# Where a step's router products and scaled output stand beside a batch's list products: one step of a fused attention and expert kernel

## The chip, the cores and the metric

The kernel runs on one core of a Trainium2 chip. The metric is the device time of one execution in microseconds, lower is better. Five engines run side by side, each through its own list of instructions in order: PE (TensorE, matrix products), DVE (VectorE), ACT (ScalarE), POOL (GpSimd) and SP (SyncE, which here only issues DMAs). They meet through semaphores. Matrix products write to PSUM banks, which DVE and ACT read; POOL works on SBUF and also issues the indirect DMAs that gather and scatter rows.

## What is computed

The reference is a linear attention with decay, followed by a mixture of experts with two levels of routing. Cut to what matters:

```python
state = gamma[None, :, None, None] * state + np.einsum('bhd,bhe->bhde', k[:, :, t], v[:, :, t])
y[:, :, t] = scale * np.einsum('bhd,bhde->bhe', q[:, :, t], state)
...
g_idx = np.argmax(x @ w_group, axis=1)             # 4 groups
e_idx = np.argmax(xg @ w_expert[g], axis=1)        # 4 experts in the group
h = np.maximum(xg[mask_e] @ w1[g, e], 0.0)
out[tok_idx] = combined[:, None] * (h @ w2[g, e])  # combined: the two softmax weights
```

Sizes: batch 4, 8 heads, 768 positions, head width 64. The attention's output is 3072 rows of 512, each of which goes through one of 16 experts (512 to 1024 to 512).

## The kernel before

**Stages.** The attention is done in 12 steps (`attention`, loop over i), each with two chunks of 128 positions. A step computes the scores of the next step (`score_mm`, L235, masked on DVE into `pf` at L247), the share of the carried state in the output (`state_out`, L286), the share of the step's own keys and values (`value_out`, L299) and the new state (`state_mm`, L261). Both shares are summed in two PSUM banks `op`, of a ring of two with the tag "mid". `out_x` (L311, DVE) multiplies them by the decay into `xt`, the scaled output. `logits_mm` (L319, PE) multiplies the `xt` of the step before by the router's weights, ACT copies the result to `ls` (L324), and `select_mm` (L332) brings it into the order of tokens. `trans_mm` (L345) transposes `xt`, ACT copies it to `xr` (L353), and SP stores it into the array `xd` in HBM (L356).

**Routing.** Six batches of four chunks are routed, beside the attention, by `route`: the choice of group and expert on DVE (L385 to L403), ranks by matrix products on PE (L436, L438), weights on DVE and POOL. From the places, `spread` makes one-hot marks `hot` (L485, DVE) and entries `yT` (L501, POOL). `tally` (L522, PE: four list products for each batch) adds them up in the PSUM bank `log`, and DVE adds that to `lists` (L529). The fourth batch is tallied in step 10, and this completes the first list for the 2048 rows so far (expert 0, called early).

**After that tally**, `beside(10, 5)` makes the first list's ids and weights with DVE (`tokens`: L534, L535, written to `mt`), issues the gather of these rows from `xd` on POOL (`gather`, L775, into `xg`), and prepares a sum `pre` for later (`known`, L541). In step 11 `xtrans` transposes the gathered rows on PE (L793). It stands behind step 11's value products and ahead of the router products of step 10, the ranks of the fifth batch and the transposes. Thereafter the first expert's layers start (L840), and fifteen further rounds over experts follow.

**What sets the order.** Nothing is scheduled by a planner: the order on each engine is that in which the Python code writes the instructions. Between engines only the tracked dependencies count. Two of them matter here. `state_out` of step 11 writes into the `op` banks of step 10, so it waits until L311 has read them. And L793 waits for the gather's DMA. `vs` (L192) and `wl` (L753) in the rows are POOL's other work, the scaled values and the low part of the split weights; `wf` at L739 is a load of weights by SP.

Of the kernel before, what the change touches and what calls it, by code (L numbers as in the profile page):

```python
# [106 lines left out]
class Kernel:  # L107
# [961 lines left out]
    def attention(self, extra, beside):  # L1069

        self.setup()
        for o in "qB0 kB0 vB0 q1 k1 v1 q2 k2 w0 c0".split():
            n, us = int(o[-1]), {"A": (0,), "B": (1,)}.get(o[1], (0, 1))
            if o[0] == "c":
                self.nc.sync.dma_start(self.rest, self.a_cst[:, C_REST:])
            elif o[0] == "w":
                self.nc.sync.dma_start(self.wr[:, :, 0:20], self.a_wr.rearrange("p (k e) -> p k e", k=4))
            else:
                self.load(o[0], n, us)

        def scores(i, u):
            if i < NS2:
                self.score_mm(i, u)
                self.score_mask(i, u)

        scores(0, 0)
        self.keys_mm(0, (0,), (self.log, self.log))
        self.vprep(0)
        self.decay_first()
        self.outs(0)  # L1090
        self.value_out(0, 0)
        scores(0, 1)
        self.keys_mm(0, (1,), (self.log, self.log))
        self.state_mm(0, 0)
        self.load("v", 2)
        self.load("k", 3)
        for i in range(NS2):
            last = i == NS2 - 1
            if i == 10:
                self.route_steps(99, True)  # L1100
                self.spread(3)
            if not last:
                self.vprep(i + 1)
            beside(i, -1)
            if i + 1 < NC:
                self.decay_next(i + 1)
            beside(i, 0)
            if i:
                if i > 2:
                    self.outs(i)  # L1110
                if i > 1:
                    scores(i + 1, 0)
                if i % 2 and not last:
                    self.select_late()
                if i in (5, 7, 9):
                    self.tally()
                if i > 2:
                    self.state_out(i, 0)
                if last:
                    self.select_late()  # L1120
                if i > 1:
                    self.state_out(i, 1)
                if i < NS2 - 2:
                    self.select_late()
                if i % 2 == 0:
                    self.route_steps(99, True)
                if i > 1:
                    scores(i + 1, 1)
            self.load("q", i + 3)
            self.load("v", i + 3)  # L1130
            if i % 2:
                self.route_steps(99)
            beside(i, 2)
            if i:
                self.value_out(i, 0)
            self.value_out(i, 1)
            if i:
                self.state_mm(i, 0)
            self.state_mm(i, 1)
            self.state_copy(i)  # L1140
            if i == 10:
                self.select_late()
                self.tally()
                beside(i, 5)
            beside(i, 4)
            if i:
                self.logits_mm(i - 1, 1 if last or i % NC == NC - 2 or i + 1 in KEYED else 2)
            self.out_x(i)
            if i < 2:
                scores(i + 1, 0)  # L1150
                scores(i + 1, 1)
            if i in (4, 6, 8):
                self.spread(i // 2 - 2)
            if last:
                self.route_steps(1, True)
                self.route_steps(99)
            beside(i, 1)
            if not last:
                banks = (self.log, self.sh[0]) if i < 2 else None
                if i == 0:  # L1160
                    self.keys_mm(1, (0,), banks)
                    self.outs(1)
                    self.state_out(1, 0)
                    self.state_out(1, 1)
                    self.keys_mm(1, (1,), banks)
                else:
                    self.keys_mm(i + 1, banks=banks)
                if i == 1:
                    self.outs(2)
                    self.state_out(2, 0)  # L1170
                self.load("k", i + 4)
            if i:
                late = i + 1 in KEYED or i % NC == NC - 2
                self.trans_mm(i - 1, late=late)
                if late:
                    self.late = i - 1
                else:
                    del self.st[i - 1]
            beside(i, 3)
            if i % 2 and not last:  # L1180
                self.route_steps(99, True)
            if i == 1:
                self.const_pieces()
            if last:
                extra(i)
            if i and i % 2 == 0:
                self.steps.append(self.route(i // 2 - 1))
            if not last:
                extra(i)
# [261 lines left out]
```

## Time and profile before

| | |
|---|---|
| time, median of 3 runs | 407.74 us (406.2 to 408.5) |
| the profiled execution | 407.63 us, of which the span from the first to the last instruction is 405.9 us |
| PE busy | 391.5 us, 96% of the span |
| DVE busy | 295.5 us, 73% |
| ACT busy | 223.4 us, 55% |
| POOL busy | 169.1 us, 42% |
| mean granted clock of TensorE | 0.989 of full speed |

Times inside the trace count from the span's start. The attention takes the first 107 us or so, the experts the rest. A granted clock of 1.00 is 2.4 GHz and 0.50 is 1.2 GHz; the mean over a stretch tells how much of it lay at the lower level.

### The profile page before, as it was taken

Reading aid. Unit: us, or ns where it says so; the run is one execution under the profiler, and the core shown is the slowest. Engines: PE = TensorE matmul, PEld = TensorE weight load, DVE = VectorE, ACT = ScalarE, POOL = GpSimd, SP = SyncE. Lnnn points to the kernel's source line nnn. Section 1 sums busy time; section 2 is a strip of 40 time slices with the busy share of each in tenths; the row PEclk is TensorE's granted clock in tenths of the full one; section 3 lists DMA queues with packets and bytes.
Section 4 is the critical chain, followed back from the end, with each engine's and each line's share of the span. In section 5 each row is a group of like instructions: output and inputs, shape, how many; then the busy total and the mean of one; then the engine's idle time right before and its main releaser. Section 6 shows DMA issues by size and latency. Waiting matters only on the chain.

```text
span 405.9 us, 13868 instructions
## 1 busy us (share of the span) xinstructions
PE 391.5 (96%) x5809; PEld 326.0 (80%) x5841; DVE 295.5 (73%) x483; ACT 223.4 (55%) x340; POOL 169.1 (42%) x172
## 2 busy tenths in 40 slices
PE   9998999998889999999999999999999999999992
PEld 5888988987769978586979888797887978879792
DVE  4575776867789979886758686777878778788620
ACT  3233535534545656555556666576766767667520
POOL 4551768668374707141507143360523505232001
PEclk9999999999999999999999999999999999999997
DMA  7999899986754997776777787879788897797000
GB/s 265 354 350 351 297 338 332 322 296 183 226 196 163 336 371 256 266 255 247 240 268 263 256 276 265 308 281 307 270 284 309 292 320 270 256 351 261 9 31 36
DMA packets 39507, 107.13 MB, mean 264 GB/s; under 512 B 12116, under 2 KB 12244, under 8 KB 32276
## 3 DMA queue, kind: packets, MB, share of 16 engines
q1 hardware_dynamic: 29760, 93.57, 66.3%
q0 software_dynamic: 9536, 12.63, 9.1%
q8 instruction: 47, 0.77, 0.8%
q14 instruction: 16, 0.13, 0.1%
q10 hardware_dynamic: 148, 0.03, 0.0%
HBM read 94.18 MB, written 13.20 MB: 265 GB/s over the span
## 4 chain that ended last, share of the span: by engine, by line
PE 46%; issue 35%; POOL 12%; DVE 3%; ACT 1%; DMA 1%; POOLq 0%; SPq 0%; ACTq 0%; DVEq 0%
PE hps L840 11%; POOL out L999 6%; PE yps L875 6%; PE op L299 5%; PE sh L235 4%; POOL xg L775 4%; PE yps L922 3%; PE op L286 2%; PE sh L345 2%; PE stp L261 2%; PE yps L925 2%; PE tpx L793 1%; PE sh L220 1%; PE sh L319 1%; PE log L332 1%
## 5 line engine op out<-in xcount | busy, mean ns | idle before, releaser
L753 DVE TENSOR_TENSOR wl<-wf,wh 128x1024 bf16<-128x1024 f32 x120 | 145.3, 1220 | 36.6 <-ACT wh L751 36.3
L751 ACT ACTIVATE wh<-wf 128x1024 f16<-128x1024 f32 (+1 forms) x136 | 133.6, 1002 | 0.3 <-DMA wf<-w2p 0.3
L840 PE MATMUL hps<-xbl,wh 128*128 128x128 f16 (+16 forms) x544 | 128.6, 249 | 0.0
L840 PE MATMUL hps<-xbh,wl 128*128 128x0 bf16 x544 | 125.8, 241 | 0.0
L840 PE MATMUL hps<-xbh,wh 128*128 128x0 bf16 x544 | 125.8, 241 | 0.0
L999 POOL DMA_INDIRECT out<-yo,mt x30 | 39.7, 1322 | 157.3 <-ACT yo L981 119.3
L840 PEld LDWEIGHTS <-wh 128*128 128x128 f16 x1088 | 94.9, 98 | 1.0 <-issue 0.2
L925 PEld LDWEIGHTS <-wh 128*128 128x128 f16 x768 | 47.1, 97 | 22.9
L775 POOL DMA_INDIRECT xg<-xd,mt x30 | 54.2, 1807 | 13.1 <-PE tpx L793 4.5
L845 ACT ACTIVATE hh<-hps 128x256 bf16<-128x256 f32 (+16 forms) x68 | 34.2, 503 | 43.7 <-PE hps L840 43.1
L840 PEld LDWEIGHTS <-wl 128*128 128x128 bf16 x544 | 53.2, 98 | 0.7
L247 DVE TENSOR_TENSOR pf<-sh,tri 128x512 f32<-128x512 f32 x48 | 30.6, 685 | 21.9 <-PE sh L235 8.1
L795 ACT ACTIVATE xbh<-tpx 128x512 bf16<-128x512 f32 (+14 forms) x32 | 16.7, 523 | 48.9 <-PE tpx L793 48.9
L848 DVE SCALAR_TENSOR_TENSOR hl<-hps,hh 128x216 f16<-128x216 f32 (+15 forms) x64 | 36.6, 574 | 4.1 <-ACT hh L845 3.7
L922 PE MATMUL yps<-wh,hl 128*128 128x512 f16 x96 | 36.4, 379 | 0.0
L922 PE MATMUL yps<-wh,hh 128*128 128x512 f16 x96 | 36.4, 379 | 0.0
L922 PE MATMUL yps<-wl,hh 128*128 128x512 bf16 x96 | 36.3, 378 | 0.0
L925 PEld LDWEIGHTS <-wl 128*128 128x128 bf16 x384 | 24.2, 97 | 11.4
L818 DVE TENSOR_TENSOR xbl<-tpx,xbh 128x512 f16<-128x512 f32 (+14 forms) x32 | 19.1, 597 | 18.3 <-ACT xbh L795 18.3
L192 POOL TENSOR_TENSOR vs<-lv,cst 128x512 f32<-128x512 f32 x24 | 24.6, 1046 | 14.0 <-DMA lv<-qkv 10.1
L925 PE MATMUL yps<-hl,wh 128*128 128x108 f16 (+11 forms) x384 | 29.1, 198 | 0.0
L925 PE MATMUL yps<-hh,wh 128*128 128x0 bf16 x384 | 26.6, 190 | 0.0
(194 smaller groups left out, 602.2 us busy)
## 6 DMA issues: line engine op xcount, KB each, us to landing
wf<-w1p SPq DMA_DIRECT2D x28, 1024.0 KB, 7.5
wf<-w2p SPq DMA_DIRECT2D x28, 1024.0 KB, 6.9
lq<-qkv SPq DMA_DIRECT2D x24, 256.0 KB, 5.5
lk<-qkv SPq DMA_DIRECT2D x24, 256.0 KB, 5.4
lv<-qkv SPq DMA_DIRECT2D x24, 256.0 KB, 5.9
xd<-xr SPq DMA_DIRECT2D x22, 256.0 KB, 4.4
wf<-w1p SPq DMA_DIRECT2D x16, 256.0 KB, 5.7
wf<-w2p SPq DMA_DIRECT2D x16, 256.0 KB, 5.5
```

What stands on the lines that cost most here:

```text
L192: self.nc.gpsimd.tensor_tensor(o, v, g, ALU.mult)
L247: nc.vector.tensor_tensor(o, sc, tri, ALU.mult)
L751: nc.scalar.activation(u["wh"][i][:, cs], u["wf"][i][:, cs], AF.Copy)
L753: (eng or nc.vector).tensor_tensor(u["wl"][i][:, cs], u["wf"][i][:, cs], u["wh"][i][:, cs], ALU.subtract)
L775: nc.gpsimd.indirect_dma_start(out=xg[0:r, i, :], out_offset=None, in_=self.xd[0:n, :], in_offset=bass.IndirectOffsetOnAxis(ap=mt[0:r, i, ...
L840: nc.tensor.matmul(o, l[:, k, fs], m, start=(n == 0), stop=(n == 11), skip_group_check=True)
L845: nc.scalar.activation(hh[:, f, 0:W], hv[:, :, 0:W], AF.Relu)
L848: nc.vector.scalar_tensor_tensor(*rest)
L875: nc.tensor.matmul(ps[0:r, :], l[:, k, ts], m[k], start=(n == 0), stop=(n == 23))
L922: nc.tensor.matmul(big, h[:, k, 0:P], w[k], start=(n == 0), stop=(n == 23))
L925: nc.tensor.matmul(o, w[k][:, d * P:d * P + P], m, start=(n == 0 and d == 0), stop=(n == 23), skip_group_check=True,)
L999: s = nc.gpsimd.indirect_dma_start(out=self.out, out_offset=bass.IndirectOffsetOnAxis(ap=mt[0:r, i, 0:1].bitcast(U32), axis=0), in_=yo[0:r ...
```

## The change

In step 10, the list products of the fourth batch with everything that hangs on them (the list sum, the ids and weights, the gather's issue, the prepared sum) are written behind the router products of step 9 and the scaled output of step 10, no longer ahead of them. Nothing is added or removed.

```diff
             if i == 10:
                 self.select_late()
-                self.tally()
-                beside(i, 5)
             beside(i, 4)
             if i:
                 self.logits_mm(i - 1, 1 if last or i % NC == NC - 2 or i + 1 in KEYED else 2)
             self.out_x(i)
+            if i == 10:
+                self.tally()
+                beside(i, 5)
```

On DVE, in step 10 behind the masks of step 11's scores (`pf`), the order before:

```order
L247 TENSOR_TENSOR pf<-sh_119,tri 128x512 [waits Activation_49]
L529 TENSOR_TENSOR lists<-lists,log 128x160 [waits PE_49]
L534 SCALAR_TENSOR_TENSOR mt<-lists 128x1 [waits DVE_49]
L535 TENSOR_REDUCE mt<-lists 128x1
L541 SCALAR_TENSOR_TENSOR pre<-lists 128x1
L311 TENSOR_TENSOR xt<-op,gx 128x512 x2
L385 TENSOR_REDUCE m<-log 128x20 [waits PE_49]
```

and on the same engine at the same place now:

```order
L247 TENSOR_TENSOR pf<-sh_119,tri 128x512 [waits Activation_49]
L311 TENSOR_TENSOR xt<-op,gx 128x512 [waits PE_49] x2
L529 TENSOR_TENSOR lists<-lists,log 128x160 [waits PE_49]
L534 SCALAR_TENSOR_TENSOR mt<-lists 128x1 [waits DVE_49]
L535 TENSOR_REDUCE mt<-lists 128x1
L541 SCALAR_TENSOR_TENSOR pre<-lists 128x1
L385 TENSOR_REDUCE m<-log 128x20 [waits PE_49]
```

The two multiplications of xt went ahead of the list sum, the ids, the weights and the prepared sum.

On PE, in step 10 behind the state products (`stp`) and the selection (`log<-rest,ls`), as a difference:

```order
 L261 MATMUL stp<-vs,kk 64x64 x16
 L332 MATMUL log<-rest,ls 128x20 x2
+L319 MATMUL sh_117<-xt,wr 32x256 x4
 L522 LDWEIGHTS hot
 L522 MATMUL log<-yT,hot 128x160
...
-L319 MATMUL sh_117<-xt,wr 32x256 x4
 L345 MATMUL sh_118<-ident,xt 128x128 x4
```

The four router products went ahead of the four list products (the pairs of L522).

On PE, in step 11, the place where the gathered rows are read; it is the same before and now:

```order
L299 MATMUL op<-pf,vs 64x128 x7
L806 TENSOR_LOAD ecols [waits DVE_49]
...
L793 MATMUL tpx<-ident,xg_80 128x128 [waits DMASW0_49]
L793 MATMUL tpx<-ident,xg_80 128x128 x3
L319 MATMUL sh_117<-xt,wr 32x256 x4
L436 LDWEIGHTS stri
L436 MATMUL log<-oh,stri 128x80 [waits DVE_49]
```

Nothing moved here: L793 waits for a DMA that POOL issued, the gather, and the router and rank products stand behind it. On POOL and SP no instruction changes its place either.

## Rows read from the trace of the kernel before

**Rows 1.** Stretches: length, busy us (x instructions) per engine, clock, DMA share, GB/s.
```profile
core 0: us, PE busy (x) PEld busy (x) DVE busy (x) ACT busy (x) POOL busy (x), PEclk, DMA share, GB/s
110.00:120.00 10.00, 8.29 (x107) 6.34 (x108) 8.88 (x33) 5.44 (x9) 7.85 (x16) 1.00 0.76 230
120.00:390.00 270.00, 270.00 (x3357) 222.55 (x3386) 211.23 (x262) 170.42 (x237) 94.09 (x61) 1.00 0.76 263
```

**Rows 2.** Timeline of step 10: start, length, engine, line, out<-in, count [idle before <-releaser].
```profile
92.51 2.47 DVE L247 TENSOR_TENSOR pf<-sh,tri 128x512 f32<-128x512 f32 x4
...
94.56 2.04 POOL L192 TENSOR_TENSOR vs<-lv,cst 128x512 f32<-128x512 f32 x2
94.65 0.44 PE L522 MATMUL log<-yT,hot 128*128 128x160 bf16 x4 [0.38 <-POOL yT L501]
...
95.02 0.64 PE L319 MATMUL sh<-xt,wr 128*32 128x256 f32 x8
95.12 0.32 DVE L529 TENSOR_TENSOR lists<-lists,log 128x160 f32<-128x160 f32 x1
...
95.56 0.15 DVE L535 TENSOR_REDUCE mt<-lists 128x1 f32<-128x3 f32 x1
...
95.59 1.09 PE L345 MATMUL sh<-ident,xt 128*128 128x128 f32 x8
95.62 0.99 DVE L541 SCALAR_TENSOR_TENSOR pre<-lists 128x1 f32<-128x1 f32 x1
...
96.54 1.28 DVE L311 TENSOR_TENSOR xt<-op,gx 128x512 f32<-128x512 f32 x2
96.78 1.28 POOL L775 DMA_INDIRECT xg<-xd,mt  x1 [0.18 <-issue]
...
97.96 0.66 PE L286 MATMUL op<-lq,V 64*64 64x128 f32 x14 [0.20 <-DVE xt L311]
```

**Rows 3.** Timeline of PE alone in step 11, and the first layer's first product.
```profile
99.70 3.56 PE L299 MATMUL op<-pf,vs 128*64 128x128 f32 x32
103.20 0.68 PE L793 MATMUL tpx<-ident,xg 128*128 128x128 f32 x4
...
107.82 0.22 PE L840 MATMUL hps<-xbl,wh 128*128 128x128 f16 x1
```

**Rows 4.** The gathered tile: landing from 96 to 104 us, SP's DMAs there, landing overall.
```profile
DMA to landing us min/median/max: 5.8/5.8/5.8
...
96.95 0.81 SPq L356 DMA_DIRECT2D xd<-xr  x2
97.82 1.93 SPq L739 DMA_DIRECT2D wf<-w1p  x4
...
DMA to landing us min/median/max: 3.4/6.7/21.7
```

**Rows 5.** Timeline of PE in step 9, at the full clock.
```profile
83.32 1.97 PE L299 MATMUL op<-pf,vs 128*64 128x128 f32 x32
85.12 1.08 PE L261 MATMUL stp<-vs,kk 128*64 128x64 f32 x28
```

**Rows 6.** Stretches around the fall of the clock, columns as in rows 1.
```profile
94.00:98.00 4.00, 2.74 (x29) 1.70 (x29) 3.64 (x8) 2.42 (x6) 3.82 (x4) 1.00 0.34 126
99.00:100.00 1.00, 1.00 (x22) 0.80 (x23) 0.49 (x2) 0.17 (x2) 1.00 (x2) 0.94 0.93 180
103.00:104.00 1.00, 1.00 (x12) 0.60 (x12) 0.84 (x2) 0.09 (x1) 0.00 (x0) 0.86 0.86 315
```

**Rows 7.** Timeline of DVE and POOL: POOL behind the gathers, and another gather.
```profile
105.63 0.24 POOL L476 TENSOR_SCALAR tile<-sf 128x4 f32<-128x4 f32 x1 [5.27 <-DVE sf L453]
...
120.69 0.15 DVE L1338 COPY mt<-final 128x1 int32<-128x1 int32 x1
...
121.27 1.10 POOL L775 DMA_INDIRECT xg<-xd,final  x1 [1.10 <-DVE mt L1338]
```

**Rows 8.** Stretches with other pauses of PE, columns as in rows 1.
```profile
36.00:38.00 2.00, 0.78 (x26) 0.65 (x24) 1.53 (x6) 0.24 (x1) 0.00 (x0) 1.00 1.01 354
398.00:399.00 1.00, 0.15 (x4) 0.00 (x1) 0.00 (x0) 0.34 (x1) 0.47 (x2) 1.00 0.17 45
400.00:401.00 1.00, 0.00 (x0) 0.00 (x0) 0.00 (x0) 0.00 (x0) 0.00 (x0) 0.62 0.64 258
```

## The prediction, made before the changed kernel ran

> **What bounds the kernel now.** I read the stretches first. From 120 us to 390 us TensorE (PE) is busy in all 270 us at the full clock [rows 1], so whatever time the attention stage gives up or saves in front of that arrives at the end undiminished. The change lies in step 10 of 12, around 92 to 98 us, so I then went through that window instruction by instruction, asking of each PE pause what ended last before it.
>
> There are two pauses. PE stands 0.38 us in front of the tally's list products until POOL has written their entries. Later the state products of step 11 (L286) wait for xt, the scaled output of step 10: they need the PSUM banks that xt reads. VectorE (DVE) finishes xt at 96.54 + 1.28 = 97.82, and PE goes on at 97.96. xt is late because DVE first takes the list sum, the ids and pre; pre alone is 0.99 us [rows 2]. In the four microseconds from 94 to 98 PE is busy 2.74, idle 1.26 [rows 6].
>
> The next thing is the clock. The granted clock falls from 2.4 to 1.2 GHz at about 99.88 (a mean of 0.94 over that microsecond is 0.12 us at one half) and is back at about 103.28 (0.86, so 0.28 us at one half) [rows 6]. In this stretch lie the 32 value products of step 11: 99.70 to 103.20 is 3.50 us, where the same 32 products in step 9 took 85.12 - 83.32 = 1.80 [rows 3, 5].
>
> The third thing is the gather of the first list's rows (L775 on POOL). It is issued at 96.78 and lands 5.8 us later, at 102.58; the transposes that read it (L793) start at 103.20, straight behind the value products [rows 2 to 4]. So before the change the gather has only 0.62 us of slack, and this is hidden in every list of waits.
>
> **The change, part by part.** *xt goes ahead of the list sum on DVE.* The masks end at 92.51 + 2.47 = 94.98; xt then runs 95.0 to 96.3, and its matmuls were done before. The state products that wait for its second half can go on at about 96.4 instead of 97.96: 1.5 us earlier. From there to the value products PE needs 99.70 - 97.96 = 1.74 us, so these start at 98.2 [rows 2, 3].
>
> *The router products go ahead of the list products on PE.* They take about 0.57 us (95.02 to the next start 95.59), start where PE stood idle, and end after the entries are written; the 0.38 us wait disappears and the transposes behind start 0.4 us earlier. They end before xt does, so this adds nothing to the 1.5 us. Its copies on ScalarE also come earlier, and nobody waits for them.
>
> *The clock.* PE's idle time between 94 and 98 is filled but for about 0.2 us, so I take it that the fall at 99.88 goes: the 32 products take 1.80 us, and PE stands in front of L793 at 98.2 + 1.8 = 100.0 instead of 103.20. If the gather were there, the change would bring 3.2 us.
>
> *The ids and the gather go back.* DVE now takes the list sum at 96.3. In before the ids and weights were done 95.56 + 0.15 - 95.12 = 0.59 us after the list sum began, which is 96.9 now instead of 95.71. In before POOL was busy with vs until 96.60, so the old lead was worth little. Now DVE's result comes last. The trace does not show this gather waiting for DVE; the nearest row is the gather at 121.27, which began 0.43 us after the copy that released it (120.69 + 0.15 = 120.84) [rows 2, 7]. I take 97.3, 0.5 us later than 96.78; with no delay behind DVE it is 96.9. By the 5.8 us of this very transfer it lands at 103.1. The weight splits behind the gather on POOL move back with it and cost nothing: POOL then waits 5.27 us for DVE [rows 7]. SyncE's order is unchanged; its writes of xr and the weight loads behind them come some 0.4 us earlier, together with the same contention for the gather.
>
> So L793 starts at about 103.1 instead of 103.20. PE waits there for 3.1 us in order, and the router products, rank products and transposes that stand behind it cannot pass it. From L793 to the first layer's products is 107.82 - 103.20 = 4.62 us of PE work in order, unchanged [rows 3]. **The 3.2 us are given back to the gather: the sum so far is -0.1 us.** For the gather I keep 3.4 us, the shortest landing of any in this trace, and 6.7, the median, as the ends [rows 4]: 103.1 becomes 100.7 or 104.0, -2.5 or +0.8.
>
> *A new idle stretch costs clock.* PE is now idle for 3.1 us in one piece. The trace brackets this: 1.22 us in one piece at 36 to 38 us left the clock at 1.00; after 1.26 us in pieces it fell; and after the last product at about 398.15 it fell at about 400.24 (0.62 is 0.76 us at one half), two microseconds into the idle [rows 6, 8]. A fall here is therefore likely. A low stretch like the one in the trace, filled with PE work, costs 3.50 - 1.80 = 1.7 us [rows 3, 5]; if part of it passes while PE still waits, less, and none if there is no fall. I take 1.3, nearer the upper end since the work behind L793 is nearly all PE's, and 0 to 1.7 as the bounds.
>
> The Trainium skill, "TensorE: Matmul & The Clock Gate", section "HAM oscillation — how this bites in real kernels", says that bursts of products with a long DMA wait between them start cold again each time. By that rule the cold start is certain here and the sum is towards +1.6; the trace has a wait of 1.22 us without a fall and one of 1.26 with one, so it agrees only in part.
>
> **Sum.** -0.1 + 1.3 = +1.2 us on the profiled execution's 407.63 us (span 405.9 and 1.7 around it): **408.8 us**. The median of the three runs, 407.74, is 0.1 above that execution. What a measurement of this kernel can tell from no change is about 0.5%, 2.0 us.
>
> **Rivals.** *No fall.* The gather still sets L793, but the clock stays up, or PE's waiting overlaps the whole low stretch. Then -0.1 remains, 407.5 us. For it: 1.22 us idle without a fall. Against it: the new idle time is over twice as long. Chance 0.18.
>
> *The gather lands early.* Its 5.8 us were shared with two stores of xr and four weight loads [rows 4]; if it took 3.4, L793 would start at 100.7: -2.5 us, 405.1 us. Against it: the loads come earlier still and are in flight again. Chance 0.07. The Trainium skill, "DMA: Bandwidth & Descriptors", section "Anatomy of one DMA — SWDGE (gpsimd) path", gives about 2.0 us plus the bytes at 436 GB/s; for 128 rows of 2 KB that is an estimate of 2.6 us, by which PE would not wait at all and the gain would be 3.2. No gather in the trace is that quick.
>
> *Slower: a second low stretch.* The low stretch begins while PE still waits, shows little work itself, and a second follows, over the end of attention and the first layer. Another 1.7 us makes +2.9, 410.5 us. It decides once more than 4.2 us of PE work run at one half, since each costs half of itself. For it: more pauses follow soon (PE is busy 8.29 of the 10 us from 110 [rows 1]). Against it: in the trace a single stretch with full work ended it. Chance 0.15.
>
> *The change does not do what it says.* The order of the instructions shows that it does; I give this nothing.
>
> **How the numbers follow.** Forecast 0.60 (408.8, by itself 407.6 to 409.7: the clock's 0 to 1.7 and the gather's issue 0.4 us sooner or a little later), no fall 0.18, early gather 0.07, second stretch 0.15. The range 406.8 to 410.5 takes in the forecast, no fall with the earliest issue, and a landing of 6.7 us with a full low stretch (+2.5, 410.1); it leaves out the early gather and the upper half of the second stretch. Faster by over 0.5% needs the early gather: 0.06. Slower by over 0.5% is the second stretch and a small part of the forecast with a late landing: 0.18. Within 0.5%: 0.76.
>
> **What would show it.** xt ending near 96.3 and the state products near 96.4; the value products of step 11 in 1.8 us; the gather issued at 96.9 to 97.3; a PE pause of about 3 us in front of L793, ended by the gather and not by a product; L793 at 102.9 to 103.4; then a clock of one half over the transposes and router products and L840 beginning at about 109 instead of 107.82. I am wrong if L793 starts before 102 (then the gather was slow only because of its company), or if the clock stays up behind the pause.

## The result, and the profile after

The changed kernel takes 410.39 us in the median of 7 runs (409.49 to 411.97), the kernel before 407.47 us in the median of 7 (406.2 to 409.09). The ratio is 1.0054, with a 95% interval of 1.0028 to 1.008. Two further comparisons on other occasions gave 1.009 (1.0056 to 1.0125) and 1.0057 (1.0032 to 1.0082). By the medians the kernel became slower by 2.9 us here and by 3.2 and 2.0 us on the two other occasions. (The ratios on record are estimates of their own and not quotients of the medians; here that quotient is 1.0072.) The forecast had the sign and the mechanism, and the time lies within its range, but only 0.1 us under the upper end: the likeliest case was worth +1.2 us.

The timeline of the changed kernel's steps 10 and 11 answers to [rows 2, 3]. The columns are start, length, engine, line, out<-in, count, and in brackets the idle time before and what ended it.

```profile
92.78 1.10 PE L261 MATMUL stp<-vs,kk 128*64 128x64 f32 x32
...
94.73 2.05 POOL L192 TENSOR_TENSOR vs<-lv,cst 128x512 f32<-128x512 f32 x2
...
95.07 1.27 DVE L311 TENSOR_TENSOR xt<-op,gx 128x512 f32<-128x512 f32 x2
...
96.19 0.87 PE L286 MATMUL op<-lq,V 64*64 64x128 f32 x16
96.26 0.30 DVE L529 TENSOR_TENSOR lists<-lists,log 128x160 f32<-128x160 f32 x1
...
96.71 0.14 DVE L535 TENSOR_REDUCE mt<-lists 128x1 f32<-128x3 f32 x1
96.78 0.14 DVE L541 SCALAR_TENSOR_TENSOR pre<-lists 128x1 f32<-128x1 f32 x1
...
97.09 1.28 POOL L775 DMA_INDIRECT xg<-xd,mt  x1 [0.32 <-DVE pre L541]
```

The same view for PE alone, further on:

```profile
98.13 1.97 PE L299 MATMUL op<-pf,vs 128*64 128x128 f32 x32
103.33 0.66 PE L793 MATMUL tpx<-ident,xg 128*128 128x128 f32 x4 [3.23 <-DMA xg<-xd,mt]
103.91 0.64 PE L319 MATMUL sh<-xt,wr 128*32 128x256 f32 x8
...
104.64 1.93 PE L345 MATMUL sh<-ident,xt 128*128 128x128 f32 x8
...
109.46 0.22 PE L840 MATMUL hps<-xbl,wh 128*128 128x128 f16 x1
```

The scaled output comes early (95.07, in before 96.54), the 32 value products take 1.97 us and no longer 3.56, and then PE stands 3.23 us until the gather has landed. L793 starts at 103.33, where it was 103.20. All that was saved is given back here. Behind it the eight transposes of L345 take 1.93 us, and 1.09 in [rows 2]. The stretches say why; their columns are as in [rows 1], the clock stands behind POOL's instructions:

```profile
104.00:105.00 1.00, 1.00 (x15) 0.59 (x16) 0.18 (x1) 0.92 (x2) 0.00 (x0) 0.83 0.00 0
105.00:108.00 3.00, 3.00 (x20) 2.33 (x18) 2.76 (x7) 1.26 (x3) 2.10 (x5) 0.50 0.25 89
108.00:109.00 1.00, 1.00 (x12) 0.84 (x9) 0.33 (x1) 0.48 (x2) 1.00 (x1) 0.96 0.67 254
```

The clock is at one half, 1.2 GHz, from 104.66 (0.83 is 0.34 us at one half) to 108.08, 3.4 us, all of it under work. So L793 to L840 takes 109.46 - 103.33 = 6.13 us instead of 4.62, and L840 starts 1.64 us later than in [rows 3]. The landing of the gather answers to [rows 4]:

```profile
DMA to landing us min/median/max: 6.2/6.2/6.2
```

The list of PE's waits (us in total, times, longest) begins with the gather; further down, behind L840, it has a pause without a releaser:

```profile
PE tpx L793 <- DMA xg<-xd,mt: 3.2, 1, 3.2
...
PE yps L875 <- issue: 0.5, 1, 0.5
```

The span of this execution is 408.5 us, 2.6 longer than before's; 1.64 of them are there at L840. The other 1.0 arises behind it, and it is not the change's: from L840 to the end of the span the changed kernel takes 299.0, 297.9 and 299.1 us in its three profiled executions, and the kernel before 298.1 and 299.1 in its two. The stretch behind L840 thus differs by 1 us between executions of either kernel.

### The profile page after: what moved, and what is told of

The parts are those of the page before. It is cut to its first block, busy times and chain, and to the rows that moved or that the text cites. A ratio compares the mean times of both kernels' runs of the same rounds, so it can differ in the third digit from the quotient of the medians.

```text
span 408.5 us, 13840 instructions
## 1 busy us (share of the span) xinstructions
PE 390.1 (95%) x5781; PEld 326.0 (80%) x5841; DVE 295.4 (72%) x483; ACT 222.9 (55%) x340; POOL 166.5 (41%) x172
## 4 chain that ended last, share of the span: by engine, by line
PE 42%; issue 35%; POOL 10%; DVE 6%; DMA 3%; ACT 1%; POOLq 0%; SPq 0%; DVEq 0%; ACTq 0%
PE hps L840 11%; POOL out L999 6%; PE yps L875 6%; PE op L299 4%; PE sh L235 4%; POOL xg L775 4%; PE yps L922 2%; PE sh L345 2%; PE op L286 2%; PE yps L925 2%; PE stp L261 2%; DMA xg<-xd,mt 2%; PE sh L220 1%; DVE pf L247 1%; DVE wl L753 1%
## 5 line engine op out<-in xcount | busy, mean ns | idle before, releaser
L840 PE MATMUL hps<-xbl,wh 128*128 128x128 f16 (+16 forms) x544 | 128.7, 249 | 0.3 <-DVE xbl L818 0.3
L840 PE MATMUL hps<-xbh,wh 128*128 128x0 bf16 x544 | 125.9, 241 | 0.4 <-issue 0.4
L840 PE MATMUL hps<-xbh,wl 128*128 128x0 bf16 x544 | 125.9, 241 | 0.0
L840 PEld LDWEIGHTS <-wh 128*128 128x128 f16 x1088 | 95.0, 98 | 1.9 <-issue 1.2
L775 POOL DMA_INDIRECT xg<-xd,mt x30 | 52.0, 1734 | 13.3 <-issue 5.5
L840 PEld LDWEIGHTS <-wl 128*128 128x128 bf16 x544 | 53.2, 98 | 0.7
L925 PE MATMUL yps<-hh,wl 128*128 128x0 bf16 x384 | 26.6, 190 | 1.3
L922 PE MATMUL yps<-wl,hh 128*128 128x512 bf16 x72 | 27.2, 378 | 0.0
```

The costliest lines, as they stand in the source:

```text
L775: nc.gpsimd.indirect_dma_start(out=xg[0:r, i, :], out_offset=None, in_=self.xd[0:n, :], in_offset=bass.IndirectOffsetOnAxis(ap=mt[0:r, i, ...
L840: nc.tensor.matmul(o, l[:, k, fs], m, start=(n == 0), stop=(n == 11), skip_group_check=True)
L922: nc.tensor.matmul(big, h[:, k, 0:P], w[k], start=(n == 0), stop=(n == 23))
L925: nc.tensor.matmul(o, w[k][:, d * P:d * P + P], m, start=(n == 0 and d == 0), stop=(n == 23), skip_group_check=True,)
```

## Experiments

The steps ahead of step 10 are fed by DMAs, and the first state product of step 10 (L261) starts anywhere from 90.96 to 96.09 us in the traces below. That moves whole executions by microseconds, and intervals of 12 runs still reach 0.2 to 0.3% to either side. So each trace is also measured from that product. The last three columns carry the rest of the argument: the start of L840 after L261, the same less that of the kernel before in its second execution, and the measured difference of the medians. For the kernel before, as profiled in front, the count begins at this row:

```profile
92.62 1.10 PE L261 MATMUL stp<-vs,kk 128*64 128x64 f32 x32
```

| kernel | L261 | L793 | L840 | L840 - L261 | against 14.62 | medians |
|---|---|---|---|---|---|---|
| before, as profiled in front | 92.62 | 103.20 | 107.82 | 15.20 | +0.58 | |
| before, again | 92.68 | 102.70 | 107.30 | 14.62 | 0 | |
| changed | 92.78 | 103.33 | 109.46 | 16.68 | +2.06 | +2.9 |
| changed, again | 92.39 | 103.09 | 110.28 | 17.89 | +3.27 | +3.2 |
| changed, third time | 92.93 | 103.73 | 109.78 | 16.85 | +2.23 | +2.0 |
| fill | 96.09 | 106.41 | 110.97 | 14.88 | +0.26 | +0.6 |
| loads early | 93.07 | 102.46 | 108.58 | 15.51 | +0.89 | -0.7 |
| output only | 90.96 | 101.49 | 107.58 | 16.62 | +2.00 | +0.3 |
| output only, again | 92.31 | 102.77 | 107.37 | 15.06 | +0.44 | +0.3 |
| router products only | 93.37 | 104.25 | 108.85 | 15.48 | +0.86 | +1.0 |
| read late | 95.09 | 105.74 | 107.80 | 12.71 | -1.91 | -1.6 |
| read late, again | 92.87 | 103.55 | 105.61 | 12.74 | -1.88 | -1.9 |
| before, read late | 92.20 | 104.00 | 106.04 | 13.84 | -0.78 | -0.9 |
| read late, loads early | 94.27 | 104.32 | 106.36 | 12.09 | -2.53 | -1.5 |

**Both kernels again.** The kernel before, once more with a profile:

> The kernel before once more, unaltered, for a second profile. The listed mean clocks of its other runs lie mostly at 0.993 to 0.997, that of the first profile at 0.989. Theory (the fall of the clock at 99.88 us was one of few): no stretch at one half between 99 and 104 us, the value products of step 11 take 1.8 us, PE then pauses about 1 us in front of L793, which the gather releases, and L793 starts 10.0 to 10.2 us behind the first state product of step 10 (L261) instead of 10.58. Rival (it falls every time): 10.6 us, no pause, and a stretch at one half.

The changed kernel, twice more:

> The changed kernel once more, unaltered. Theory (gather, then clock): the transposes of the gathered rows (L793) are released by the gather at 103.1 to 103.5, PE idle 3.0 to 3.4 us in front of them, one stretch of the granted clock at one half behind them, and 2 to 3 us over before. Rival (the new order itself makes a wait later on): the further 1.1 us that the first profile lost between 124 and 134 us, beginning with a pause of about 0.6 us inside the first layer of the second short list, comes again at the same place; if it belonged to that execution, the shift against before stays near 1.5 us there.

> The changed kernel once more, beside the three below on the same chip. The theory that its price is one or two stretches at half clock behind the new pause expects 2 to 3.3 us over before, L793 at 10.4 to 10.8 us behind the first state product of step 10 and L840 at 16.6 to 17.9. A rival, that most of its price was the occasion, expects under 1 us over before.

The one execution of before took 408.13 us; the median of the 29 runs beside it is 408.73. It tells more than a repeat should. Its pauses of PE in step 10 are those of the profiled one, 0.38, 0.68 and 0.20 us against 0.38, 0.69 and 0.20, and yet its clock does not fall. PE's timeline of it:

```profile
92.68 1.10 PE L261 MATMUL stp<-vs,kk 128*64 128x64 f32 x32
...
97.43 0.40 PE L286 MATMUL op<-lq,V 64*64 64x128 f32 x2 [0.68 <-DVE xt L311]
98.03 0.66 PE L286 MATMUL op<-lq,V 64*64 64x128 f32 x14 [0.20 <-DVE xt L311]
...
99.77 1.97 PE L299 MATMUL op<-pf,vs 128*64 128x128 f32 x32
102.70 0.66 PE L793 MATMUL tpx<-ident,xg 128*128 128x128 f32 x4 [0.96 <-DMA xg<-xd,mt]
...
107.30 0.22 PE L840 MATMUL hps<-xbl,wh 128*128 128x128 f16 x1
```

and a stretch of it, at the full clock:

```profile
100.00:110.00 10.00, 7.99 (x111) 6.64 (x109) 7.63 (x25) 6.03 (x13) 4.04 (x7) 1.00 0.73 233
```

The value products take 1.97 us already here, and L793 waits 0.96 us for the gather. The gather is what L793 waits for before the change too; that it was not so in [rows 3] came from the fallen clock of that one execution. How common is it? A stretch of 3.42 us at one half takes 0.5 x 3.42 / 406 = 0.004 off an execution's mean clock. Of the 94 runs of before in the three later comparisons 11 have a mean clock of 0.992 or less, the others 0.993 to 0.997. Of the 26 runs of the changed kernel 25 have 0.992 or less. This count doesn't say where in an execution the clock was low (the profiled execution of the filled kernel below has 0.990 from a stretch between 80 and 90 us, ahead of step 10, and none behind it), but it fits the traces: the usual kernel before has no low stretch here, and the changed one nearly always has. A third trace with the same work and the same pauses in front, that of the kernel before with late reading below (0.39, 0.68 and 0.20 us), has no fall either.

In the changed kernel's second execution the clock fell while PE still waited, and did not come back for nearly seven microseconds:

```profile
103.09 1.12 PE L793 MATMUL tpx<-ident,xg 128*128 128x128 f32 x4 [3.38 <-DMA xg<-xd,mt]
...
110.28 0.22 PE L840 MATMUL hps<-xbl,wh 128*128 128x128 f16 x1
```

```profile
102.00:103.00 1.00, 0.00 (x0) 0.00 (x0) 0.00 (x0) 0.00 (x0) 0.00 (x0) 0.63 1.03 399
103.00:109.00 6.00, 5.91 (x38) 3.92 (x38) 3.20 (x7) 2.17 (x4) 2.35 (x5) 0.50 0.20 71
109.00:110.00 1.00, 1.00 (x13) 1.00 (x10) 0.07 (x1) 0.65 (x2) 1.00 (x1) 0.96 0.54 205
```

That is 6.8 us at one half without a rise between, twice the 3.4 of the other two traces, and L793 to L840 takes 7.19 us. It is the rival with the second low stretch, its price 2.6 us over the 4.6 at the full clock. In the third execution the pause is the longest, and the clock fell as it ended, at about 103.72 (0.86 is 0.28 us at one half):

```profile
103.73 1.11 PE L793 MATMUL tpx<-ident,xg 128*128 128x128 f32 x4 [3.48 <-DMA xg<-xd,mt]
```

```profile
103.00:104.00 1.00, 0.27 (x2) 0.27 (x3) 0.00 (x0) 0.00 (x0) 0.00 (x0) 0.86 0.80 307
```

**Fill: PE kept at work in the pause.** The changed kernel with 14 products of constants ahead of L793, which nothing reads:

```diff
                 if place == 4 and last:
+                    fill = self.pp.tile([P, 512], F32, name="fill", tag="sta", bufs=1)
+                    for _ in range(14):
+                        nc.tensor.matmul(fill, self.one[:, 0:P], self.one, start=True, stop=True)
                     self.shape(ua, 4, 0, self.early_cols)
                     self.xtrans(ua, 'big', (0,), low=False)
```

> The changed kernel with 14 products of constants (128x512, 0.22 us each at the full clock, about 3.0 us) that PE works off in the pause ahead of L793; nothing reads their result. Theory: L793 still starts at about 103.3, released by the gather, but the clock stays at 1.00 behind it, the work from L793 to the first layer takes 4.6 us as in before instead of 6.2, the first layer begins at about 107.9, and the time is 1.5 us under the changed kernel, some 0.5 to 1 us over before. Rival (the clock is not what costs): the same time as the changed kernel.

Measured 407.36 us in 12 runs, 1.0016 of before (0.9995 to 1.0037), 2.6 us under the changed kernel of the same occasion (409.98). PE's timeline and the whole stretch:

```profile
103.34 3.23 PE L1271 MATMUL fill<-const-bfloat16-1.0 128*128 128x512 bf16 x14
106.41 0.62 PE L793 MATMUL tpx<-ident,xg 128*128 128x128 f32 x4
...
107.69 1.07 PE L345 MATMUL sh<-ident,xt 128*128 128x128 f32 x8
```

```profile
99.00:112.00 13.00, 13.00 (x156) 9.49 (x155) 7.83 (x25) 7.33 (x14) 7.68 (x10) 1.00 0.57 187
```

The clock stays at 1.00, the transposes take 1.07 us, and L793 to L840 takes 110.97 - 106.41 = 4.56 us. The loss but for some 0.3 to 0.6 us was the clock, and it is larger than I had expected. The filled kernel has neither the loss nor a gain, since the gather, which lands 5.9 us after its issue at 100.4, still holds L793 about where it was (10.32 us after L261, 10.55 in the changed kernel).

**Loads early: fewer transfers beside the gather.** The second half of the weight loads that SP issues here for the second expert goes out with the first half, one step earlier:

```diff
-NEXT = {(10, 0): (0, 4), (11, 0): (4, 8)}
+NEXT = {(10, 0): (0, 8)}
```

> The changed kernel, but the four weight loads that SP issues beside the gather (second half of the second expert's w1) are issued with the first four, a step earlier, so that the gather has only the two stores of xr beside it. Theory A (the gather is slow because of its company): it lands after about 4 us instead of 6.2, L793 at about 101.2, a pause of 1.1 us, no fall of the clock, about 2 us under before. Theory B (its 6 us are its own): landing within 0.5 us of 6.2, time as the changed kernel, +2 to +3 us over before.

Measured 406.12 us, 0.998 of before (0.9955 to 1.0005). The landing, and PE at L793:

```profile
DMA to landing us min/median/max: 5.0/5.0/5.0
```

```profile
102.46 0.66 PE L793 MATMUL tpx<-ident,xg 128*128 128x128 f32 x4 [2.07 <-DMA xg<-xd,mt]
```

The gather takes 1.2 us less than in the changed kernel, so these four loads cost it about that much (with late reading, below, it takes 5.3 us without them beside it and 6.3 with); the pause is still 2.07 us. Of the two theories neither was met: the landing is between the 4 us of the one and the 6.2 of the other. In this profile the clock fell behind it (L793 to L840 6.12 us):

```profile
103.00:104.00 1.00, 1.00 (x10) 0.20 (x8) 0.00 (x0) 0.60 (x1) 0.00 (x0) 0.55 0.00 0
```

But only 3 of the 12 runs have a mean clock of 0.992 or less; their median is 408.16 us, that of the 9 others 405.42. Without the fall L840 would come 4.6 us behind L793, 14.0 us after L261 and 0.6 under before, and -0.7 was measured. That the trace was of an unusual run is inferred from the mean clocks; no profile of a run without the fall was taken.

**The two halves of the change.** First the scaled output alone goes ahead:

```diff
+            beside(i, 4)
+            if i == 10:
+                self.out_x(i)
                 self.tally()
                 beside(i, 5)
-            beside(i, 4)
             if i:
                 self.logits_mm(i - 1, 1 if last or i % NC == NC - 2 or i + 1 in KEYED else 2)
-            self.out_x(i)
+            if i != 10:
+                self.out_x(i)
```

> Only the half of the change on DVE: xt ahead of the list sum, ids and pre; the router products stay behind the list products. Theory (xt ahead of the ids is what delays the gather and opens the pause): as the changed kernel, gather issued 4.3 to 4.5 us behind the first state product of step 10, a PE pause of 3 us in front of L793, a low clock behind it, 2 to 3 us over before. Rival (the router products matter): clearly less over before than the changed kernel.

> Of the change, only the scaled output goes ahead; the router products stay behind the list products. Timed again since the first interval reached from -0.3 to +0.3% while the trace was that of the changed kernel. If moving the scaled output is the whole of the change, the time is within 0.7 us of the changed kernel's on this occasion (2 to 3 us over before), with a pause of 2.8 to 3.3 us ahead of L793 and a stretch at half clock behind it. The rival, that the router products carry most of the loss, expects it within 0.7 us of before.

Measured 1.0003 of before (0.9972 to 1.0033) and 1.001 (0.9985 to 1.0035). The two profiles, L793 and the stretch behind it, first and second time:

```profile
101.49 0.66 PE L793 MATMUL tpx<-ident,xg 128*128 128x128 f32 x4 [2.81 <-DMA xg<-xd,mt]
...
103.00:104.00 1.00, 1.00 (x8) 1.00 (x7) 0.86 (x5) 0.23 (x1) 0.02 (x1) 0.50 0.23 86
```

```profile
102.77 0.65 PE L793 MATMUL tpx<-ident,xg 128*128 128x128 f32 x4 [2.74 <-DMA xg<-xd,mt]
...
104.00:105.00 1.00, 1.00 (x14) 0.96 (x14) 0.67 (x4) 0.69 (x3) 0.00 (x0) 1.00 0.32 121
```

Pauses of 2.81 and 2.74 us, and the clock fell behind the one and not behind the other. Of the 24 runs 10 have a mean clock of 0.992 or less. My expectation of 2 to 3 us over before missed: it took the fall as certain. Where it does not happen, L840 comes 0.44 us later than in before. The times divide the same way: the runs at 0.992 or less have medians of 409.82 and 410.26 us on the two occasions, the others 408.56 and 408.21, beside 408.73 and 408.67 for before. Of the second expectation the rival's number held (within 0.7 us of before), but its reason, that the router products carry most of the loss, is not borne out by the next kernel.

Then the router products alone, with the list products behind them and the scaled output last:

```diff
-                self.tally()
-                beside(i, 5)
             beside(i, 4)
             if i:
                 self.logits_mm(i - 1, 1 if last or i % NC == NC - 2 or i + 1 in KEYED else 2)
+            if i == 10:
+                self.tally()
+                beside(i, 5)
             self.out_x(i)
```

> Only the half of the change on PE: the router products ahead of the list products; xt stays behind the ids and pre. Theory: gather and xt as in before, the wait of 0.4 us in front of the list products gone and taken up again in front of the state products; within 0.3% of before. Rival (the router products matter): 1 us or more away from before.

Measured 409.71 us, 1.0017 of before (0.999 to 1.0044). PE, DVE and a stretch:

```profile
98.26 0.40 PE L286 MATMUL op<-lq,V 64*64 64x128 f32 x2 [1.41 <-DVE xt L311]
...
101.14 2.98 PE L299 MATMUL op<-pf,vs 128*64 128x128 f32 x32
104.25 0.66 PE L793 MATMUL tpx<-ident,xg 128*128 128x128 f32 x4
```

```profile
96.37 1.01 DVE L534 SCALAR_TENSOR_TENSOR mt<-lists 128x1 int32<-128x1 f32 x1
```

```profile
100.00:101.00 1.00, 1.00 (x17) 0.77 (x17) 0.49 (x2) 0.19 (x2) 1.00 (x2) 0.50 0.73 111
```

The router products fill the wait for POOL's entries, but xt is late, and the two pauses of before (0.38 and 0.68 us) become one of 1.41 us. The clock falls over the value products, which end with the gather's landing: no wait is left at L793, and it starts 10.88 us after L261 where before had 10.02. That gather and xt would be as in before did not hold: the gather is issued 4.31 us after L261 (4.16 before) and takes 6.5. 10 of the 12 runs have a mean clock of 0.992 or less. Neither half is distinguished from before by its time; both together are. By the traces, the one lengthens the pause at L793 to 2.8 us, and the other takes another 0.4 from what PE had to do ahead of it (value products at 5.35 us after L261, not 5.74). Behind 2.8 us the clock fell in one profile of two, behind 3.2 to 3.5 in three of three, and behind the 2.07 of early loads in the one there is; so the pause's length alone does not tell, and what decides is open.

**Read late: the pause gets work.** The changed kernel with the transposes of the gathered rows written behind the router products, ranks and transposes of step 10 and the router products of step 11:

```diff
-                if place == 4 and last:
-                    self.shape(ua, 4, 0, self.early_cols)
-                    self.xtrans(ua, 'big', (0,), low=False)
...
-                    if last:
-                        self.xlow(ua, 0)
...
             self.logits_mm(last)
+            self.shape(ua, 4, 0, self.early_cols)
+            self.xtrans(ua, 'big', (0,), low=False)
+            self.xlow(ua, 0)
             self.trans_mm(last, self.yp)
```

> The changed kernel, but the transposes that read the gathered rows stand behind the router products, ranks and transposes of step 10 and the router products of step 11, so 2.7 us of PE work run while the gather is under way. Theory: the pause in front of L793 shrinks to about 0.5 us, the clock stays up, the first layer begins at about 105.5, and the time is 2 to 2.5 us under before: the earlier xt is worth what the gather had taken back. Rival (the copies behind L793 come onto the path instead): the first layer waits some 1.4 us for them, and the time is about 1 us under before. Second rival (the gather was not what held PE): the time of the changed kernel.

> The changed kernel with the transposes of the gathered rows behind the router products, ranks and transposes, a second time. If the first result (0.42% under before) was no accident of its occasion, 1 to 2.5 us under before and 4 to 5.5 under the changed kernel, the clock at 1.00 throughout and L840 at 12.5 to 13 us behind the first state product of step 10. The rival, that the early scaled output brings nothing by itself, expects it level with before.

Measured 405.22 us, 0.9958 of before (0.9936 to 0.9981), and 406.74 us, 0.9949 (0.9925 to 0.9973), the second time 3.9 us under the changed kernel of the same occasion. PE's timeline, first time:

```profile
104.50 0.64 PE L319 MATMUL lgt<-xt,wr 128*32 128x256 f32 x8
105.74 0.66 PE L793 MATMUL tpx<-ident,xg 128*128 128x128 f32 x4 [0.60 <-DMA xg<-xd,mt]
...
107.80 0.22 PE L840 MATMUL hps<-xbl,wh 128*128 128x128 f16 x1 [0.18 <-DVE xbl L818]
```

```profile
100.00:110.00 10.00, 8.50 (x121) 7.06 (x120) 6.25 (x22) 5.90 (x11) 6.45 (x9) 1.00 0.83 279
```

The gather lands no sooner, but 2.8 us of PE's work (the pause begins at 105.74 - 0.60 = 105.14, the router products behind the value products at 102.35) now lies between the value products and L793. Of the pause 0.60 us is left, the clock stays at 1.00, and L840 comes 1.9 us sooner than in before. This version beats both kernels. Is it the late reading alone? The same move in the kernel before, without the change:

> The order of before, but the transposes of the gathered rows stand behind the router products, ranks and transposes of step 10 and the router products of step 11. It tells what the change is worth where the gather holds nobody. Theory: no wait for the gather; xt is 1.5 us later than with the change, so the first layer begins some 14 us behind the first state product of step 10 (15.2 in before, 12.7 in the kernel with the change and the late reading), about 1 us under before and 1 to 1.5 us over the kernel with both. Rival (the change brings nothing even so): the same time as the kernel with both, 1.6 us under before.

Measured 407.79 us, 0.9993 (0.9963 to 1.0022), which decides nothing by itself. In its trace nothing waits for the gather any more:

```profile
104.00 0.63 PE L793 MATMUL tpx<-ident,xg 128*128 128x128 f32 x4
```

L840 comes 13.84 us after L261, 0.8 us sooner than before and 1.1 later than with the change. So the change is worth about 1.1 us by the traces once other products stand in front of L793, and the 0.60 us still waited there keep it from more; that rests on traces alone, the two kernels were timed on different occasions.

Last, late reading and early loads together, by both edits above (the loads are the second expert's here too):

> The kernel with the late reading, and the second half of the first list's weight loads issued with the first half, so that fewer loads run beside the gather. If only the gather's landing matters, the wait of 0.6 us ahead of L793 goes, L840 is at 12.0 to 12.7 and the time 0 to 0.7 us under the kernel with the late reading alone. If the early loads are worth something of their own (the changed kernel with early loads was 3.9 us under the changed kernel, of which its trace showed 1.2 to 2.4), 1.5 to 3 us under it.

Measured 407.16 us, 0.9967 of before (0.9942 to 0.9993). The wait at L793 goes, but by time it is not better than the late reading alone (406.74): the 0.6 us of the trace is too small to be told. That early loads are worth 1.5 to 3 us in themselves is not borne out.

## Why the prediction was right, and where it was too small

**The scaled output comes 1.5 us earlier: right (1.63).** L311 starts 95.07 - 92.78 = 2.29 us after L261 and not 96.54 - 92.62 = 3.92. The value products take 1.97 us at the full clock, as said.

**The gather goes back: right in kind, too large by 0.35 us, and the landing too short by 0.4.** I forecast its issue at 97.3. It is 97.09, and from L261 on it is 4.31 us against 4.16. The ids and weights were done when forecast (96.71 + 0.14 = 96.85, and 96.9 was said); the gather began 0.24 us behind them and not the 0.43 taken from another gather. In all three traces of the changed kernel the landing is longer than the 5.8 us I took, 6.2, 6.4 and 6.5. The output-only kernel, with 6.1 and 6.2, and the router-only kernel with 6.5 have it too, and the filled one (5.9) hardly; what it is stays open. The two errors cancel: L793 was forecast at 103.1, and is at 103.33, after a pause forecast at 3.1 and measured at 3.23. The early landing, the rival of a gain, is out: even with the four loads gone it took 5.0 us.

**"So before the change the gather has only 0.62 us of slack": the step that failed first.** It was read from one execution whose clock had fallen. In the usual one the gather is already late by 0.96 us and L793 is at 10.02 us after L261, not 10.58. So the -0.1 at L793 was the right difference to the wrong reference: against the usual kernel before it is 10.55 - 10.02 = +0.5. The 3.2 us that a present gather would have brought were to one half (3.50 - 1.80 = 1.7) the low clock of that execution. The mean clock in the table of before, 0.989, stood among the values that 11 of 94 runs have; one execution could not tell that.

**The new idle stretch costs clock, +1.3: right in kind, the term mis-sized.** It was 6.13 - 4.62 = 1.5 in one trace, 16.85 - 10.80 - 4.62 = 1.4 in the third, both within the bounds of 0 to 1.7, and 7.19 - 4.62 = 2.6 in the second, where the rival of a second stretch came in, as one long stretch. Its price of +2.9, reckoned on the profiled execution of before, stands against 17.89 - 15.20 = +2.69 in that trace. I gave it 0.15; one trace of three, and mean clocks down to 0.982, suggest that it was more. Filling the pause took 2.6 us off the time, which shows the term by itself. The rival without a fall, 0.18, is not seen in any of the three traces; of the 26 runs one, at a mean clock of 0.996 and 407.92 us, may be it.

The Trainium skill, "TensorE: Matmul & The Clock Gate", section "HAM oscillation — how this bites in real kernels", has the products behind a long DMA wait start cold each time. The traces agree in part: behind the pauses of 3.38 and 3.48 us the transposes of L793 run at one half (1.12 and 1.11 us), behind the 3.23 us they still run at the full clock (0.66) and the fall comes 1.3 us into the work, and behind the 2.74 us of the output-only kernel there is none.

**The sum.** On the reference that the forecast used, the profiled execution of before, L840 moved by 16.68 - 15.20 = +1.48 us, where +1.2 was said. On the usual one, reference +0.5 and clock +1.5 are +2.06 (with one stretch), +3.27 with two; the three differences of medians are +2.9, +3.2 and +2.0. The forecast's +1.2 lacks the half microsecond of the reference and part of the clock. Slower by over 0.5% had 0.18 and is where the ratio of 1.0054 lies, though its interval begins at 1.0028; with the reference put right, the likeliest case would have been -0.1 + 0.6 + 1.3 = +1.8, just under 0.5% itself. That the time fell within the range is in part luck: with two stretches in place of one it is at the range's end, and the median of the third occasion, 410.65, is beyond it. The spread given for the forecast alone, 407.6 to 409.7, is a slip at its lower end: no loss of clock and an issue 0.4 us sooner make 407.1.

## To carry to other kernels

Here the work saved ahead of an in-order wait for a DMA became idle time, and the idle time cost clock on top: look for what can stand between the early work and the wait before moving the early work (with other products ahead of the transposes this kernel is 0.4 to 0.5% faster than before, of which the change has some 1.1 us by the traces; without them it is 0.5 to 0.9% slower). A slack read from one execution is worth only as much as that execution is usual: its mean clock beside those of the other runs is a first sign of whether a low stretch in it belongs to the kernel, though it doesn't say where the stretch lies. Where start times scatter by microseconds, measure two traces from the same instruction near the change.

## What the hardware showed that was not expected

The same program with the same pauses in front (0.38, 0.68 and 0.20 us) kept the full clock in one execution and lost it in another, and pauses of 2.74 and 2.81 us differed in the same way, while one of 2.07 us (early loads) was followed by a fall. After a fall the low stretch was 3.4 us in most traces and 6.8 in one.

A DVE instruction on one column takes 0.14 to 0.19 us, but 0.99 in [rows 2] (pre, 95.62 to 96.61) and 1.01 with the router products only (L534, above). In [rows 2] it ends when POOL's vs ends, 94.56 + 2.04 = 96.60; in the changed kernel pre starts at 96.78, when vs has ended (94.73 + 2.05), and takes 0.14. With the router products only, L534 ends at 96.37 + 1.01 = 97.38, and vs at 97.37:

```profile
95.32 2.05 POOL L192 TENSOR_TENSOR vs<-lv,cst 128x512 f32<-128x512 f32 x2
```

The Trainium skill, "SBUF — State Buffer", section "SBUF: two separate sides", says that DVE and GpSimd share one pair of ports, which a GpSimd instruction, or a DVE instruction with two inputs in SBUF, holds to its end while the other waits. The rows agree: pre and L534 have two inputs in SBUF and end with a vs instruction of 1.04 us, while xt, which has one in PSUM, runs beside vs in the changed kernel (95.07) in 1.27 us and behind it in [rows 2] in 1.28. So of the 1.63 us that the scaled output gained, some 0.85 is this small instruction no longer held up ahead of it.
